# Attention and a two-layer network on one core: a shorter float64 conversion, unread matmuls, and four instead of eight weight pieces in float32

## The chip, the core and the metric

The kernel runs on one core of a Trainium2 chip. The metric is the device time of one execution in microseconds. Engines are named as the profile names them: PE is TensorE (PEld its weight loads), DVE is VectorE, ACT is ScalarE, POOL is GpSimd, SP is SyncE, which issues the transfers.

## The reference

Causal attention over 4 batches, 12 heads, 448 positions and 64 columns a head, and then a two-layer network on its output, 1792 tokens of 768 columns, with 2048 hidden columns. The two weight matrices are given in float64, the rest in float32; the output is float32.

```python
scores = q @ k.transpose(0, 1, 3, 2) / sqrt(64)
scores = where(triu(ones((448, 448)), k=1), -1e9, scores)
attn = exp(scores - max(scores)); attn = attn / (sum(attn) + 1e-9)
x = (attn @ v).transpose(0, 2, 1, 3).reshape(1792, 768)
h = x @ w_in                                   # w_in  768 x 2048, float64
g = where(h > 0, h, exp(minimum(h, 0)) - 1)
out = (g @ w_out).astype(float32)              # w_out 2048 x 768, float64
```

## The kernel before

The 448 positions of each batch are cut into four chunks of 112. Tile g is chunk g of all four batches, 448 tokens. The kernel goes through the four tiles: the two layers of tile g run on PE interleaved with the attention of tile g + 1, in proportion to their costs. Only the attention of tile 0 (`first_pair`) stands alone, at the start. It goes by six pairs of heads. For each pair, scores of both heads go into two PSUM tiles `sc`; DVE adds the mask and finds the row's extreme (L267); ACT takes the exponential (L271); DVE or POOL multiplies by the reciprocal of the sum (L352); PE transposes the result into a PSUM tile `tr` (L286); ACT or DVE copies that to `at` (L289, L290); PE multiplies with v into the PSUM tile `av` (L299).

The layers want x as the sum of two float32r parts. `split_x` makes `xh`, a copy on ACT (L314), and `xl`, the rest, on DVE (L316). Weights are cut into 34 pieces: 16 of w_in (768 elements a partition) and 18 of w_out (12 of 768 and 6 of 512). In tile 0, `weights` loads a piece as 64-bit words and converts it: ACT takes the absolute value of the high half (L545), DVE bounds and scales it (L546), DVE masks the sign (L549), DVE shifts and ors (L552), ACT scales the low half (L556), POOL adds the two as integers (L559). The float32 piece `w` is written to DRAM (L562), from where the later tiles load it. Then it is split into two float32r parts, `wh` by a copy on ACT (L571) and `wl` by a subtraction on DVE or POOL (L572), and a product is three matmuls (L581 to L583: high x high, high x low, low x high). In tile 0 the first `PLAIN` = 8 pieces of w_in are not split: they meet an unsplit copy `xf` of x in one float32 matmul (L597). Between the layers, ACT and DVE form g and split it (L604 to L610); L627 copies an output tile out of PSUM.

Buffers come from rings: four PSUM tiles of tag `p` (for `sc` and `tr`), one of tag `av`, three of tag `hp` (both layers); in SBUF eight of tag `w6` (64-bit words, split weights, and from tile 2 on split q and k) and five of tag `w`. In each ring the n-th tile takes the place of the one n - bufs before it, once that is read for the last time. `Ring.free_at` gives tiles out in the order in which they were asked for, except under tag `p`.

The order of all work is found ahead of time by a list scheduler in the kernel's own Python (`Plan`). `add` records an instruction or a lump of them, with the tiles that it reads and writes, an estimated cost, and for some a second or third engine that may do it. PE's lumps carry due times; those of other work follow backwards from what needs it, transfers with a lead that grows with their size. `run` then starts, again and again, the work that can start first, the earliest due among those within 0.12 us, and takes another engine when that would end sooner by the estimates. Each engine thus has one fixed order on the chip; the estimates decide that order and nothing else.

Of the kernel before, what the change touches and what calls it, by code (L numbers as in the profile page):

```python
# [11 lines left out]
U32 = mybir.dt.uint32  # L12
# [5 lines left out]
CP = 112  # L18
# [50 lines left out]
class Plan:  # L69
# [4 lines left out]
    def __init__(self):  # L74
        self.works = []

    def add(self, ways, reads=(), writes=(), due=None, size=0.0, hold=()):


        if isinstance(ways, tuple):  # L80
            ways = [ways]
        full = lambda x: [(b, None) if isinstance(b, Buf) else b for b in x]
        reads, writes = full(reads), full(writes)
        w = Work(ways, size, due, reads, writes, hold)
        meet = lambda a, b: a is None or b is None or a == b
        for b, key in reads:
            w.preds |= {o for o, k, wr in b.uses if wr and meet(k, key)}
        for b, key in writes:
            w.preds |= {o for o, k, wr in b.uses if meet(k, key)}
        for b, key in reads:  # L90
            b.uses.append((w, key, False))
        for b, key in writes:
            b.uses.append((w, key, True))
        for b in w.bufs:
            b.left += 1
        for p in w.preds:
            p.succs.append(w)
        self.works.append(w)
        return w
# [87 lines left out]
def attention_moe_kernel(ctx, tc, qk, v, w_in, w_out, out):  # L187
# [27 lines left out]
    def f32(ap):  # L215
        return ap.bitcast(F32)
# [9 lines left out]
        nm=4, su=4, rr=4, hp=3, p=4, av=1,  # L226
    )

    PLAIN = 8

    SPLIT = 2

# [2 lines left out]
        ring = rings.setdefault(tag, Ring(BUFS[tag], in_order=tag != "p"))  # L235
        return ring.new(lambda: pool.tile(shape, dtype, tag=tag, name=name or tag, bufs=BUFS[tag]))

    def pe(cost, fn, reads, writes, due, hold=()):
        plan.add(("PE", cost, fn, False), reads, writes, due, hold=hold)

    def act(n, fn, more=0.05):
        return ("ACT", more + 0.84e-3 * n, fn, False)
# [4 lines left out]
    def pool(n, fn, rate=2.3e-3):  # L247
        return ("POOL", 0.1 + rate * n, fn, True)

    def dma(kb, rows, fn, reads, writes):  # L250
        plan.add(("SP", 0.35 + 0.5e-3 * rows, fn, False), reads, writes, size=kb / 260.0)

# [12 lines left out]
    def softmax(sc, a, key, c, n, nm, su, x, sums=True):  # L265

        plan.add(dve(n, lambda: nc.vector.tensor_tensor_reduce(  # L267
            out=a()[:, c], in0=sc()[:, c], in1=mask[:, S - n:], op0=ALU.add, op1=ALU.min,
            scale=-scale, scalar=3.0e38, accum_out=nm()[:, x:x + 1],
        )), [(sc, key)], [(a, key), (nm, x)])  # L270
        plan.add(act(n, lambda: nc.scalar.activation(  # L271
            a()[:, c], a()[:, c], AF.Exp, bias=nm()[:, x:x + 1], scale=-1.0, accum_out=su()[:, x:x + 1] if sums else None,
        ), 0.28 if sums else 0.11), [(nm, x)], [(a, key)] + [(su, x)] * sums)

    def reciprocals(su, rr):
        plan.add(dve(4, lambda: nc.vector.tensor_scalar_add(rr(), su(), EPS), more=0.2), [su], [rr])
        plan.add(dve(4, lambda: nc.vector.reciprocal(rr(), rr()), more=0.21), [], [rr])

    def transposes(blocks, due):

        tr, at = new("p", [CP, S], name="tr"), new("at", [CP, S])
        w = CP * len(blocks)

        def fn():
            for x, (a, i) in enumerate(blocks):
# [17 lines left out]
        pe(0.2 * len(what), fn, [vb] + [at for two in what for _, at, _ in two], [(av, b)], due)  # L303

    def split_x(g, p, av):
        if g == 0:
            x = xf[p] = new("gl" if p % 2 else "gh", [P, S], name="xf")
            plan.add([
                act(S, lambda: nc.scalar.activation(x(), av(), AF.Copy)),
                dve(S, lambda: nc.vector.tensor_copy(x(), av())),  # L310
            ], [av], [x])
        xh = new("xh", [P, S], F32R)
        xl = new("xl", [P, S], F32R)
        plan.add(act(S, lambda: nc.scalar.activation(xh(), av(), AF.Copy)), [av], [xh])  # L314
        plan.add(
            dve(S, lambda: nc.vector.tensor_tensor(out=xl(), in0=av(), in1=f32(xh()), op=ALU.subtract)), [av, xh], [xl]  # L316
        )
        xt[g, p] = xh, xl

    first = [(new("gh", [P, S], name="q0"), new("gl", [P, S], name="k0")) for _ in range(NP)]  # L320

    def first_pair(p, due):
        q0, k0 = first[p]
        v0 = new("v", [CP, B, 2, D], name="v0")
        for t, x in enumerate((q0, k0)):
            src = qk[:, 2 * p:2 * p + 2, :, t, :CP].rearrange("b h d c -> (h d) b c")
            dma(224, P * B, lambda x=x, src=src: nc.sync.dma_start(
                out=x().rearrange("p (b c) -> p b c", b=B), in_=src
            ), [], [x])
        for half in range(2):  # L330
            src = v[:, p, :, half, 0].rearrange("b c d -> c b d")
            dma(112, CP * B, lambda half=half, src=src: nc.sync.dma_start(out=v0()[:, :, half], in_=src), [], [(v0, half)])
        sc = [new("p", [CP, S], name="sc") for _ in range(2)]
        a = [new("a", [CP, S]) for _ in range(2)]
        nm, su, rr = (new(x, [CP, 2 * B]) for x in ("nm", "su", "rr"))

        def scores():
            for b in range(B):
                for half in range(2):
                    d = half_of(half)  # L340
                    nc.tensor.matmul(sc[half]()[:, chunk(b)], q0()[d, chunk(b)], k0()[d, chunk(b)], start=True, stop=True)
        pe(0.9, scores, [q0, k0], sc, due, [*a, nm, su, rr])
        for half in range(2):
            for b in range(B):
# [12 lines left out]
        at = [transposes([(a[half], b) for b in range(B)], due + 3.0) for half in range(2)]  # L357
# [170 lines left out]
    def weights(g, key):  # L528
# [7 lines left out]
        if g == 0:  # L536
# [4 lines left out]
            wf = lambda: w()[:, :n]  # L541
            dma(n * P, P, lambda: nc.sync.dma_start(
                out=r()[:, :n].rearrange("p k c w -> p k (c w)"), in_=src.bitcast(U32)
            ), [], [r])
            plan.add(act(size, lambda: nc.scalar.activation(wf(), f32(high()), AF.Abs)), [(r, 1)], [w])  # L545
            plan.add(dve(size, lambda: nc.vector.tensor_scalar(  # L546
                wf(), wf(), MOST, REBIAS, op0=ALU.min, op1=ALU.mult
            ), 0.55e-3, 0.06, True), [], [w])
            plan.add(dve(size, lambda: nc.vector.tensor_scalar(  # L549
                high(), high(), 0x80000000, None, op0=ALU.bitwise_and  # L550
            ), 0.55e-3, 0.06, True), [], [(r, 1)])
            plan.add(dve(size, lambda: nc.vector.scalar_tensor_tensor(  # L552
                out=wf().bitcast(U32), in0=wf().bitcast(U32), scalar=3, in1=high(),
                op0=ALU.logical_shift_left, op1=ALU.bitwise_or,
            ), port=True), [(r, 1)], [w])
            plan.add(act(size, lambda: nc.scalar.activation(  # L556
                low().bitcast(I32), low(), AF.Copy, scale=2.0 ** -29
            )), [], [(r, 0)])
# [3 lines left out]
            dma(n * 64, P, lambda: nc.sync.dma_start(out=k(), in_=wf()), [w], [k])  # L562
        else:
            k = kept[key]
            dma(n * 64, P, lambda: nc.sync.dma_start(out=w()[:, :n], in_=k()), [k], [w])
        if g == 0 and key[0] == "i" and key[1] < PLAIN:
            wt[(g, *key)] = (w,)
            return
        t = whl[key] if g == 0 else new("w6", [P, 2, KT, P], F32R, "whl")
        wh, wl = (lambda: t()[:, 0]), (lambda: t()[:, 1])  # L570
        plan.add(act(size, lambda: nc.scalar.activation(wh()[:, :n], w()[:, :n], AF.Copy)), [w], [(t, 0)])  # L571
        sub = lambda eng: lambda: eng.tensor_tensor(  # L572
            out=wl()[:, :n], in0=w()[:, :n], in1=f32(wh()[:, :n]), op=ALU.subtract
        )
# [63 lines left out]


    FIRST, EACH, SLOW, TAIL = 4.0, 3.0, 1.3, 5.0  # L640
    for p in range(NP):
        first_pair(p, FIRST + EACH * p)
    t = FIRST + EACH * NP + 4.0
# [49 lines left out]
```

## Time and profile before

| what | us |
|---|---|
| median of 3 runs | 675.41 |
| the three runs | 675.42, 673.94, 675.41 |
| the profiled execution | 673.43 |
| its span, first to last instruction | 671.6 |
| PE busy in it | 651.4 (97%) |
| PE weight loads | 552.6 (82%) |
| ACT busy | 457.5 (68%) |
| DVE busy | 437.0 (65%) |
| POOL busy | 132.8 (20%) |

The difference between the time of the profiled execution and its span lies before its first and after its last instruction. Busy times are sums over the whole span; matmuls overlap, and their ends are modelled, so PE's share is not a share of its peak. The mean granted TensorE clock is 0.986 of full speed (2.4 GHz). A float32 matmul shows as two records, a float32r matmul as one.

### The profile page before, as it was taken

The page shows a single profiled execution, that of the slowest core. Times are in us where ns is not written, and L with a number is a line of the kernel's source. Part 1 is how long each engine was busy: PE and PEld are TensorE (multiplying, and loading weights), DVE is VectorE, ACT ScalarE, POOL GpSimd, SP SyncE. Part 2 cuts the span into 40 slices and gives each one's busy share as a digit, 9 for nine tenths or more (in the row PEclk, how much of TensorE's full clock was granted, in tenths as well). Part 3 has the DMA queues.
Part 4 walks back from the last instruction along what each step waited for, and adds up shares of the span by engine and source line. Part 5 has one row for each costly group of instructions (what it writes and reads, how often), then busy time and mean ns, then how long its engine had stood idle before and what let it go on. Part 6 is the DMA issues. An engine that isn't in the chain of part 4 may idle for free.

```text
span 671.6 us, 11799 instructions
## 1 busy us (share of the span) xinstructions
PE 651.4 (97%) x4176; PEld 552.6 (82%) x4176; DVE 437.0 (65%) x998; ACT 457.5 (68%) x1004; POOL 132.8 (20%) x108
## 2 busy tenths in 40 slices
PE   5899999999999999999999999999999999999997
PEld 4655577878888888888888888888888999999996
DVE  5788998999977676875552678677374526554200
ACT  6998888997857888776662788788566436664210
POOL 1343333534341231111020123111111100000000
PEclk9899997999999999999999999999999999999999
DMA  9999566979869353553647446363443643324210
GB/s 231 283 365 354 182 213 172 318 221 280 300 189 300 113 171 87 163 157 106 203 140 212 121 126 191 101 184 109 128 121 104 216 145 94 102 88 115 77 28 27
DMA packets 83578, 114.80 MB, mean 171 GB/s; under 512 B 39104, under 2 KB 59072, under 8 KB 83520
## 3 DMA queue, kind: packets, MB, share of 16 engines
q1 hardware_dynamic: 83520, 114.06, 55.5%
q8 instruction: 33, 0.54, 0.3%
q14 instruction: 25, 0.20, 0.1%
HBM read 95.94 MB, written 18.09 MB: 170 GB/s over the span
## 4 chain that ended last, share of the span: by engine, by line
PE 79%; DVE 9%; ACT 7%; issue 2%; DMA 2%; SPq 0%; ACTq 0%; DVEq 0%
PE op L581 10%; PE hp L581 10%; PE op L583 10%; PE op L582 10%; PE hp L583 10%; PE hp L582 9%; PE av L452 6%; PE tr L473 6%; PE sc L422 4%; ACT a L271 3%; PE hp L597 2%; DVE whl L572 2%; DMA w_o<-w 2%; DVE w L552 1%; DVE w L546 1%
## 5 line engine op out<-in xcount | busy, mean ns | idle before, releaser
L572 DVE TENSOR_TENSOR whl<-w,whl 128x768 fp32r<-128x768 f32 (+1 forms) x114 | 107.0, 941 | 56.6 <-ACT whl L571 53.7
L581 PE MATMUL op<-gh,whl 128*128 128x448 f32 x384 | 143.4, 374 | 0.0
L583 PE MATMUL op<-gh,whl 128*128 128x448 f32 x384 | 140.7, 366 | 1.0 <-DVE whl L572 1.0
L582 PE MATMUL op<-gl,whl 128*128 128x448 f32 x384 | 140.6, 366 | 0.4 <-DVE gl L610 0.4
L571 ACT ACTIVATE whl<-w 128x768 fp32r<-128x768 f32 (+1 forms) x128 | 99.8, 796 | 48.3 <-PE op L583 31.0
L581 PE MATMUL hp<-xh,whl 128*128 128x448 f32 x336 | 127.8, 380 | 0.8 <-ACT whl L571 0.8
L583 PE MATMUL hp<-xh,whl 128*128 128x448 f32 x336 | 124.4, 370 | 1.3 <-DVE whl L572 1.3
L582 PE MATMUL hp<-xl,whl 128*128 128x448 f32 x336 | 124.2, 370 | 0.0
L271 ACT ACTIVATE a<-a,nm 112x112 f32<-112x112 f32 (+3 forms) x192 | 97.1, 520 | 31.3 <-DVE nm L267 31.2
L267 DVE CUSTOM_DVE_ANT_0 a<-sc,mask 112x112 f32<-112x112 f32 (+3 forms) x192 | 75.0, 442 | 42.6 <-PE sc L422 34.7
L559 POOL TENSOR_TENSOR w<-w,w 128x768 int32<-128x768 int32 (+1 forms) x34 | 65.7, 1933 | 98.4 <-DVE w L552 40.0
L581 PEld LDWEIGHTS op<-gh,whl 128*128 128x128 f32 x384 | 72.1, 188 | 9.5 <-issue 3.0
L583 PEld LDWEIGHTS op<-gh,whl 128*128 128x128 f32 x384 | 72.1, 188 | 8.1 <-DVE whl L572 2.0
L582 PEld LDWEIGHTS op<-gl,whl 128*128 128x128 f32 x384 | 72.2, 188 | 6.4 <-DVE gl L610 0.8
L606 DVE SCALAR_TENSOR_TENSOR hp<-m,hp 128x448 f32<-128x448 f32 x64 | 40.1, 627 | 56.0 <-ACT m L605 55.7
L581 PEld LDWEIGHTS hp<-xh,whl 128*128 128x128 f32 x336 | 63.8, 190 | 11.4 <-issue 4.4
L583 PEld LDWEIGHTS hp<-xh,whl 128*128 128x128 f32 x336 | 63.9, 190 | 7.9 <-DVE whl L572 2.1
L582 PEld LDWEIGHTS hp<-xl,whl 128*128 128x128 f32 x336 | 63.9, 190 | 5.3 <-issue 0.2
L604 ACT ACTIVATE m<-hp 128x448 f32<-128x448 f32 x64 | 34.5, 540 | 37.5 <-PE hp L583 36.5
L572 POOL TENSOR_TENSOR whl<-w,whl 128x768 fp32r<-128x768 f32 x14 | 25.9, 1852 | 135.5 <-ACT whl L571 117.8
L452 PEld LDWEIGHTS av<-at,v 112*64 112x64 f32 x864 | 41.6, 137 | 11.9 <-issue 11.0
L452 PE MATMUL av<-at,v 112*64 112x112 f32 x864 | 49.3, 263 | 0.0
(57 smaller groups left out, 859.9 us busy)
## 6 DMA issues: line engine op xcount, KB each, us to landing
w<-w_i SPq DMA_DIRECT2D x48, 384.0 KB, 3.5
w<-w_o SPq DMA_DIRECT2D x36, 384.0 KB, 3.1
w<-in_w_in SPq DMA_DIRECT2D x16, 768.0 KB, 7.7
w<-in_w_out SPq DMA_DIRECT2D x12, 768.0 KB, 5.9
k<-in_qk SPq DMA_DIRECT2D x30, 224.0 KB, 4.1
w_i<-w SPq DMA_DIRECT2D x16, 384.0 KB, 5.0
q<-in_qk SPq DMA_DIRECT2D x24, 224.0 KB, 4.6
out_t<-ob SPq DMA_DIRECT2D x24, 224.0 KB, 2.7
```

The source lines that it names most:

```text
L267: plan.add(dve(n, lambda: nc.vector.tensor_tensor_reduce(out=a()[:, c], in0=sc()[:, c], in1=mask[:, S - n:], op0=ALU.add, op1=ALU.min, sca ...
L271: plan.add(act(n, lambda: nc.scalar.activation(a()[:, c], a()[:, c], AF.Exp, bias=nm()[:, x:x + 1], scale=-1.0, accum_out=su()[:, x:x + 1] ...
L452: nc.tensor.matmul(av()[half_of(half), chunk(o["b"])], o["v"]()[:, half, i], at()[:, chunk(x)], start=i == 0, stop=i == g,)
L473: nc.tensor.transpose(tr()[:, chunk(x)], o["a"][half]()[:, chunk(i)], ident)
L559: plan.add(pool(size, lambda: nc.gpsimd.tensor_tensor(out=wf().bitcast(I32), in0=wf().bitcast(I32), in1=low().bitcast(I32), op=ALU.add)), ...
L571: plan.add(act(size, lambda: nc.scalar.activation(wh()[:, :n], w()[:, :n], AF.Copy)), [w], [(t, 0)])
L572: sub = lambda eng: lambda: eng.tensor_tensor(out=wl()[:, :n], in0=w()[:, :n], in1=f32(wh()[:, :n]), op=ALU.subtract)
L581: nc.tensor.matmul(acc(), wh()[:, k], xh(), start=first, stop=False)
L582: nc.tensor.matmul(acc(), wh()[:, k], xl(), start=False, stop=False)
L583: nc.tensor.matmul(acc(), wl()[:, k], xh(), start=False, stop=last)
L604: plan.add(act(S, lambda: nc.scalar.activation(m(), hp(), AF.Relu, scale=-1.0)), [hp], [m])
L606: plan.add(dve(S, lambda: nc.vector.scalar_tensor_tensor(out=hp(), in0=m(), scalar=-1.0, in1=hp(), op0=ALU.add, op1=ALU.max)), [m], [hp])
```

## The change

Six things change, all but one in the work of tile 0.

- Conversion of the float64 words: DVE clamps the high half to plus or minus `MOST`, ACT scales it with Prelu (positive values by `REBIAS`, negative ones by 2^32 times that, the sign landing in place after the shift), DVE shifts left by three bits. The two instructions for the sign are gone.
- `PLAIN` is 4: pieces 4 to 7 of w_in are split like the others in tile 0.
- The copy `wh` may run on ACT or on DVE, in all tiles.
- `split_x` of tile 0 copies `av` once, to `xf`; `xh` and `xl` are made from `xf`, and `xl` may run on DVE or POOL.
- `fills`: float32 products of the identity with itself into a PSUM tile that the next scores or transposes overwrite. Nothing reads them. Eight stand before the first pair's scores, due two microseconds ahead of them; two before each of the twelve transposes of tile 0, not before that pair's scores (`after`) and due one microsecond ahead of the transposes.
- The planner's estimates: `RATE` 350 for transfers of weights and 280 for others instead of 260 for all, and 0.19 instead of 0.11 us in an exponential without sums.

```diff
-    PLAIN = 8
+    PLAIN = 4
+    RATE = 350.0
...
+    def fills(n, t, due, after=None):
+        for _ in range(n):
+            pe(0.2, lambda: nc.tensor.matmul(t()[:, :CP], ident, ident, start=True, stop=True), [], [t], due, after=after)
+
-    def transposes(blocks, due):
+    def transposes(blocks, due, fill, after):
         tr, at = new("p", [CP, S], name="tr"), new("at", [CP, S])
         w = CP * len(blocks)
+        fills(fill, tr, due - 1.0, after)
...
     def split_x(g, p, av):
...
+        x = xf[p] = new("gl" if p % 2 else "gh", [P, S], name="xf")
+        plan.add([
+            act(S, lambda: nc.scalar.activation(x(), av(), AF.Copy)),
+            dve(S, lambda: nc.vector.tensor_copy(x(), av())),
+        ], [av], [x])
+        plan.add(act(S, lambda: nc.scalar.activation(xh(), x(), AF.Copy)), [x], [xh])
+        sub = lambda eng: lambda: eng.tensor_tensor(out=xl(), in0=x(), in1=f32(xh()), op=ALU.subtract)
+        plan.add([dve(S, sub(nc.vector), port=True), pool(S, sub(nc.gpsimd))], [x, xh], [xl])
...
-        pe(0.9, scores, [q0, k0], sc, due, [*a, nm, su, rr])
+        if p == 0:
+            fills(FILL[0], sc[0], due - 2.0)
+        scored = pe(0.9, scores, [q0, k0], sc, due, [*a, nm, su, rr])
...
-            plan.add(act(size, lambda: nc.scalar.activation(wf(), f32(high()), AF.Abs)), [(r, 1)], [w])
             plan.add(dve(size, lambda: nc.vector.tensor_scalar(
-                wf(), wf(), MOST, REBIAS, op0=ALU.min, op1=ALU.mult
+                wf(), f32(high()), MOST, -MOST, op0=ALU.min, op1=ALU.max
+            ), 0.55e-3, 0.06, True), [(r, 1)], [w])
+            plan.add(act(size, lambda: nc.scalar.activation(wf(), wf(), AF.Prelu, scale=REBIAS, alpha=2.0 ** 32)), [], [w])
+            plan.add(dve(size, lambda: nc.vector.tensor_scalar(
+                wf().bitcast(U32), wf().bitcast(U32), 3, None, op0=ALU.logical_shift_left
             ), 0.55e-3, 0.06, True), [], [w])
-            plan.add(dve(size, lambda: nc.vector.tensor_scalar(
-                high(), high(), 0x80000000, None, op0=ALU.bitwise_and
-            ), 0.55e-3, 0.06, True), [], [(r, 1)])
-            plan.add(dve(size, lambda: nc.vector.scalar_tensor_tensor(
-                out=wf().bitcast(U32), in0=wf().bitcast(U32), scalar=3, in1=high(),
-                op0=ALU.logical_shift_left, op1=ALU.bitwise_or,
-            ), port=True), [(r, 1)], [w])
...
-        plan.add(act(size, lambda: nc.scalar.activation(wh()[:, :n], w()[:, :n], AF.Copy)), [w], [(t, 0)])
+        plan.add([
+            act(size, lambda: nc.scalar.activation(wh()[:, :n], w()[:, :n], AF.Copy)),
+            dve(size, lambda: nc.vector.tensor_copy(wh()[:, :n], w()[:, :n]), 0.55e-3, 0.06, True),
+        ], [w], [(t, 0)])
...
+    FILL = 8, 2
```

## Rows read from the trace of the kernel before

**Rows 1.** Stretches: start:end, length, busy us of five engines, clock, DMA share, GB/s.
```profile
0.00:37.60 37.60, 26.03 (x232) 20.52 (x232) 25.51 (x137) 29.52 (x98) 10.77 (x17) 0.86 1.00 269
37.60:85.40 47.80, 47.80 (x225) 26.04 (x224) 42.27 (x99) 42.22 (x95) 18.87 (x14) 1.00 0.84 294
85.40:130.00 44.60, 42.73 (x245) 35.93 (x244) 42.09 (x79) 38.67 (x80) 19.06 (x10) 0.92 0.71 220
130.00:206.00 76.00, 74.28 (x454) 63.26 (x453) 67.30 (x126) 58.65 (x124) 29.30 (x17) 1.00 0.81 260
206.00:372.00 166.00, 165.24 (x1155) 144.29 (x1153) 103.94 (x251) 114.93 (x266) 27.39 (x25) 1.00 0.53 160
```
**Rows 2.** Chain that ended last, 37 to 75 us: start, us, what.
```profile
48.43 5.28 PE hp L597 x14
53.70 0.94 PE sc L428 x8
...
56.35 0.92 PE av L452 x16
57.27 0.92 PE tr L473 x8
```
**Rows 3.** Timeline of ACT: copies of output tiles, of the first and the last tile.
```profile
206.52 0.55 ACT L627 ACTIVATE ob<-op 128x448 f32<-128x448 f32 x1 [2.14 <-PE op L583]
...
618.44 0.55 ACT L627 ACTIVATE ob<-op 128x448 f32<-128x448 f32 x1 [1.59 <-PE op L583]
...
667.44 0.54 ACT L627 ACTIVATE ob<-op 128x448 f32<-128x448 f32 x1 [9.24 <-PE op L583]
```
**Rows 4.** Groups of PE by line, 85.4 to 206 us: count, busy, mean ns, idle before.
```profile
L452 PE MATMUL av<-at,v 112*64 112x112 f32 x144 | 8.9, 265 | 0.0
L428 PE MATMUL sc<-k,q 64*112 64x224 f32 x56 | 8.3, 377 | 0.9 <-DVE nm L267 0.6 <-ACT at L477 0.3
L473 PE MATMUL tr<-ident,a 112*112 112x112 f32 x64 | 7.8, 265 | 0.0
```
**Rows 5.** Chain that ended last, 0 to 40 us.
```profile
4.72 1.86 PE sc L341 x16
...
7.00 5.31 ACT a L271 x24
...
13.85 0.44 ACT at L289
```
**Rows 6.** Timeline of PE, 102 to 105 us; in brackets idle before and its releaser.
```profile
102.45 0.47 PE L581 MATMUL hp<-xh,whl 128*128 128x448 f32 x1 [0.53 <-ACT whl L571]
...
103.98 0.74 PE L583 MATMUL hp<-xh,whl 128*128 128x448 f32 x1 [0.79 <-DVE whl L572]
```
**Rows 7.** Two short stretches, columns as in rows 1.
```profile
14.00:20.00 6.00, 5.67 (x41) 4.91 (x42) 3.75 (x19) 3.79 (x13) 2.01 (x3) 0.51 1.22 259
104.00:108.00 4.00, 4.00 (x11) 3.61 (x12) 3.96 (x5) 2.26 (x3) 1.91 (x1) 0.50 0.97 365
```
**Rows 8.** Groups by line and shape, 0 to 206 us: conversion, split of weights and x.
```profile
L552 DVE SCALAR_TENSOR_TENSOR w<-w,w 128x768 uint32<-128x768 uint32 x28 | 26.8, 958 | 0.8
L545 ACT ACTIVATE w<-w 128x768 f32<-128x768 f32 x28 | 25.4, 909 | 0.0
L572 DVE TENSOR_TENSOR whl<-w,whl 128x768 fp32r<-128x768 f32 x20 | 21.0, 1049 | 1.1 <-ACT whl L571 0.9
L546 DVE TENSOR_SCALAR w<-w 128x768 f32<-128x768 f32 x28 | 20.3, 724 | 1.9 <-ACT w L545 1.7
L571 ACT ACTIVATE whl<-w 128x768 fp32r<-128x768 f32 x20 | 16.8, 838 | 1.9 <-POOL w L559 1.9
L316 DVE TENSOR_TENSOR xl<-av,xh 128x448 fp32r<-128x448 f32 x12 | 7.4, 619 | 4.0 <-ACT xh L314 2.4 <-PE sc L428 1.5
L314 ACT ACTIVATE xh<-av 128x448 fp32r<-128x448 f32 x12 | 6.5, 539 | 1.8 <-DVE xf L310 1.2 <-PE av L452 0.4 <-PE av L299 0.2
```
**Rows 9.** One line's instructions, whole span: duration ns min/median/max, first and last start.
```profile
L546 DVE TENSOR_SCALAR w<-w x34: 415/554/2209, 29.3 to 198.7; 128x768 f32<-128x768 f32 x28, 128x512 f32<-128x512 f32 x6
```
**Rows 10.** One line's instructions, whole span, as in rows 9.
```profile
L219 ACT ACT_TABLE_LOAD  x1: 1283/1283/1283, 0.7 to 0.7; - x1
```

More of the change, by code (lines that the diff above doesn't have):

```diff
@@ L75, in __init__, with add @@
         self.works = []
-    def add(self, ways, reads=(), writes=(), due=None, size=0.0, hold=()):
+    def add(self, ways, reads=(), writes=(), due=None, size=0.0, hold=(), after=None):
         if isinstance(ways, tuple):
@@ L93, in add @@
             b.uses.append((w, key, True))
+        if after:
+            w.preds.add(after)
         for b in w.bufs:
@@ L236, in new, with pe @@
         return ring.new(lambda: pool.tile(shape, dtype, tag=tag, name=name or tag, bufs=BUFS[tag]))
-    def pe(cost, fn, reads, writes, due, hold=()):
-        plan.add(("PE", cost, fn, False), reads, writes, due, hold=hold)
+    def pe(cost, fn, reads, writes, due, hold=(), after=None):
+        return plan.add(("PE", cost, fn, False), reads, writes, due, hold=hold, after=after)
     def act(n, fn, more=0.05):
@@ L248, in pool, with dma @@
         return ("POOL", 0.1 + rate * n, fn, True)
-    def dma(kb, rows, fn, reads, writes):
-        plan.add(("SP", 0.35 + 0.5e-3 * rows, fn, False), reads, writes, size=kb / 260.0)
+    def dma(kb, rows, fn, reads, writes, rate=280.0):
+        plan.add(("SP", 0.35 + 0.5e-3 * rows, fn, False), reads, writes, size=kb / rate)
     NG = NCH
@@ L272, in softmax @@
             a()[:, c], a()[:, c], AF.Exp, bias=nm()[:, x:x + 1], scale=-1.0, accum_out=su()[:, x:x + 1] if sums else None,
-        ), 0.28 if sums else 0.11), [(nm, x)], [(a, key)] + [(su, x)] * sums)
+        ), 0.28 if sums else 0.19), [(nm, x)], [(a, key)] + [(su, x)] * sums)
     def reciprocals(su, rr):
@@ L305, in split_x @@
     def split_x(g, p, av):
[L306 to L311, printed above, removed]
         xh = new("xh", [P, S], F32R)
         xl = new("xl", [P, S], F32R)
[L314 to L317, printed above, removed]
         xt[g, p] = xh, xl
+        if g:
+            plan.add(act(S, lambda: nc.scalar.activation(xh(), av(), AF.Copy)), [av], [xh])
+            plan.add(dve(S, lambda: nc.vector.tensor_tensor(
+                out=xl(), in0=av(), in1=f32(xh()), op=ALU.subtract
+            )), [av, xh], [xl])
+            return
+        x = xf[p] = new("gl" if p % 2 else "gh", [P, S], name="xf")
[6 more added lines that the diff above has]
+        plan.add([dve(S, sub(nc.vector), port=True), pool(S, sub(nc.gpsimd))], [x, xh], [xl])
     first = [(new("gh", [P, S], name="q0"), new("gl", [P, S], name="k0")) for _ in range(NP)]
@@ L356, in first_pair @@
             plan.add([dve(S, mul(nc.vector), port=True), pool(S, mul(nc.gpsimd), 1.9e-3)], [rr], [a[half]])
-        at = [transposes([(a[half], b) for b in range(B)], due + 3.0) for half in range(2)]
+        at = [transposes([(a[half], b) for b in range(B)], due + 3.0, FILL[1], scored) for half in range(2)]
         av = new("av", [P, S])
@@ L543, in weights @@
                 out=r()[:, :n].rearrange("p k c w -> p k (c w)"), in_=src.bitcast(U32)
-            ), [], [r])
-            plan.add(act(size, lambda: nc.scalar.activation(wf(), f32(high()), AF.Abs)), [(r, 1)], [w])
+            ), [], [r], RATE)
             plan.add(dve(size, lambda: nc.vector.tensor_scalar(
-                wf(), wf(), MOST, REBIAS, op0=ALU.min, op1=ALU.mult
-            ), 0.55e-3, 0.06, True), [], [w])
-            plan.add(dve(size, lambda: nc.vector.tensor_scalar(
-                high(), high(), 0x80000000, None, op0=ALU.bitwise_and
-            ), 0.55e-3, 0.06, True), [], [(r, 1)])
-            plan.add(dve(size, lambda: nc.vector.scalar_tensor_tensor(
-                out=wf().bitcast(U32), in0=wf().bitcast(U32), scalar=3, in1=high(),
-                op0=ALU.logical_shift_left, op1=ALU.bitwise_or,
-            ), port=True), [(r, 1)], [w])
+                wf(), f32(high()), MOST, -MOST, op0=ALU.min, op1=ALU.max
[3 more added lines that the diff above has]
+                wf().bitcast(U32), wf().bitcast(U32), 3, None, op0=ALU.logical_shift_left
+            ), 0.55e-3, 0.06, True), [], [w])
             plan.add(act(size, lambda: nc.scalar.activation(
@@ L561, in weights @@
             )), [(r, 0)], [w])
-            dma(n * 64, P, lambda: nc.sync.dma_start(out=k(), in_=wf()), [w], [k])
+            dma(n * 64, P, lambda: nc.sync.dma_start(out=k(), in_=wf()), [w], [k], RATE)
         else:
             k = kept[key]
-            dma(n * 64, P, lambda: nc.sync.dma_start(out=w()[:, :n], in_=k()), [k], [w])
+            dma(n * 64, P, lambda: nc.sync.dma_start(out=w()[:, :n], in_=k()), [k], [w], RATE)
         if g == 0 and key[0] == "i" and key[1] < PLAIN:
```

## The prediction

> **What bounds the kernel now.** I first cut the span by what TensorE computes. The table of stretches [rows 1] has the first tile's attention (0 to 37.6 us), the eight pieces of w_in that meet x in float32 (to 85.4), the other eight (to 130) and the w_out products with the rest of the second tile's attention (to 206). In the next stretch PE is busy 165.24 of 166.00 us at full clock, and no float64 word is left to convert. The change has nothing to shorten there; I leave 206 to 671.6 alone, and all that follows is about the first 206 us.
>
> "PE busy" is not to be taken at its word, because ends of matmuls are modelled and overlap. A better measure is what the products cost when nothing interrupts them. A float32 product of 448 columns is two records: 14 records in 5.28 us, 0.754 us a product [rows 2]. A three-part product: five output tiles of 16 products lie between the copies at 618.44 and 667.44, so 49.0 / 80 = 0.6125 us [rows 3]. A score record of the second tile costs 0.94 / 8 = 0.1175, a transpose 0.92 / 8 = 0.115, an av record 0.92 / 16 = 0.0575 [rows 2]. Between 85.4 and 206 there are 48 + 96 three-part products, 88.2 us, and by the counts of [rows 4] 56 x 0.1175 + 64 x 0.115 + 144 x 0.0575 = 22.2 of attention; with the last float32 product 111.2 of 120.6 us: PE loses 9.4 there. From 37.6 to 85.4 its row shows no idle at all [rows 1], so I take that stretch as PE-bound. Before 37.6 ACT is busy 29.5 us, nearly all after its first exponential at 7.00 [rows 1, 5]: ACT's queue is the chain.
>
> Where much of the 9.4 went can be seen from 85.4 to 130: DVE is busy 42.1 of 44.6 us, ACT 38.7, the granted clock is 0.92 [rows 1]. At 102 and 104 PE waits for a piece of w_in that ACT and then DVE has just split, and the clock stands at 0.50, the lower level of 1.2 GHz, right behind [rows 6, 7]. DVE sets that stretch, and PE starves.
>
> **The change, part by part.** *Conversion.* Each of 34 pieces (28 of 768 elements, 6 of 512, two thirds of the price) loses one DVE instruction: bound-and-scale, sign mask and shift-or become clamp and shift. The shift-or took 0.958 us [rows 8], so 28 x 0.958 + 6 x 0.64 = 30.7 us leave DVE. Clamp and shift are not in the trace. The nearest row is the bound-and-scale, mean 0.724 us [rows 8], median 0.554 [rows 9]; I price each like the instruction it replaces, so nothing. If one ran at the shift-or's rate it would return 34 x (0.958 - 0.724) = 8 us of DVE, if both 16. Prelu takes Abs's place on ACT, same size, 0.909 us; the other row of that size is 0.838 [rows 8], so nothing, with an end of 2.4 us less and the same more. The chain becomes DVE, ACT, DVE, POOL, one handover more, hidden as long as conversions run a piece ahead; uncovered it costs about one such instruction, 0.9 us.
>
> *PLAIN 8 to 4.* 24 products go from 0.754 to 0.6125: 3.4 us less PE. In return four more pieces are split: 4 x 0.838 on ACT and 4 x 1.049 on DVE [rows 8], 3.4 and 4.2 us. The copy half of a split may now also run on DVE: nearest row 0.554, upper end 0.958.
>
> *One copy out of PSUM.* xh and xl of the first tile are made from SBUF. The single av buffer comes free after one reader instead of three, and the six xh copies (6 x 0.539 = 3.2 us of ACT [rows 8]) need not run before 37.6: only piece 4 needs them. They go into the second stretch; xl (6 x 0.619, 3.7 on DVE) goes with them, or to POOL.
>
> *Unread products.* Eight run before the first scores, while PE waits for q and k until 4.72 [rows 5], and two before each of 12 transposes. Nearest rows: two records like av or like a transpose, 0.115 to 0.23 us a product, twice that at half clock. At 0.23 the 24 are 5.5 us of PE where PE is busy 26.0 of 37.6 [rows 1]: free while PE waits for the softmax, 5.5 if all were on the chain. What they can give: from 14 to 20 us the clock is 0.51, and ACT is busy only 3.79 of 6 [rows 7]: 2.2 us idle while PE works at half rate.
>
> *RATE* changes only the order and lead of weight loads; with no PE idle from 37.6 to 85.4 [rows 1] no load is late now, so nothing.
>
> **The sum.** First stretch: up to 2.2 from the clock and 3.2 from the moved copies; conversions that come earlier will take part of that room, so 2.5 (ends -3.0 and 5.4). From 37.6 to 206, 168.4 us: PE needs 168.4 - 9.4 - 3.4 = 155.6, so at best 12.8 go. ACT would hold 42.2 + 38.7 + 58.7 + 3.4 + 3.2 = 146.2, DVE 42.3 + 42.1 + 67.3 - 30.7 + 4.2 + 3.7 = 128.9. Two engines near 90% in one static order will still make PE wait now and then, as DVE did; I take two thirds, 8.5 (ends 0 and 12.8). Sum 11.0 us.
>
> The profiled execution took 673.43 us, its span 671.6 and 1.8 around it; the median of the runs is 675.41, 2.0 more. 673.4 - 11.0 = 662.4 by the profile, 664.4 by the median: I say 664.
>
> **A rule on ports.** The bound-and-scale has a median of 554 ns and a maximum of 2209 [rows 9]: now and then it stands behind something else. The Trainium skill, GPSIMD Engine Reference, Key points, says that POOL shares its SBUF interfaces with VectorE, and that DVE instructions in a two-port mode, or with two SBUF inputs, contend with it. By that rule copies of w moved to DVE, and xl moved to POOL, would make more such waits. The row gives a price, 2.21 - 0.55 = 1.66 us each; six more of them on the chain would take 10 us and bring the sum to 1. I count as many as now, since the mean of 0.724 already holds them.
>
> **Rivals.**
> 1. *ACT becomes the bound.* From 37.6 to 130, 92.4 us, ACT would hold 42.2 + 38.7 + 3.4 + 3.2 = 87.5. In these two stretches ACT is now filled to 88% and 87% [rows 1]; at that fill 87.5 us take 99. If the copies of w stay on ACT, nothing is won there, 2.5 before and about 1.5 behind: 671. For it: ACT's sum. Against it: the room of 30.7 us on DVE, to which copies may go.
> 2. *PSUM held by the unread products (slower).* They write the transposes' tile, so its buffer is taken right after the pair's scores. The four buffers then hold one pair's scores and transposes, and a later pair's scores wait for the copy out. The first pair takes from 4.72 to 14.29, 9.6 us, from scores to that copy [rows 5], against (37.6 - 7.0) / 6 = 5.1 us a pair now. One pair at a time would add 5 x 4.5 = 22.5 us: 675.4 - 8.5 + 22.5 = 689. It decides from 6.8 us a pair, where 5 x 1.7 eats the other 8.5. Against it: score buffers come free after the masking, so two pairs can be under way.
> 3. *A table load for each Prelu.* The trace has one load, 1.283 us at the start, and none after it [rows 10]. If Prelu and the exponential needed different tables, 34 pieces would load twice: 87 us of ACT, of which its idle time up to 206 (206 - 169 = 37 us) hides some: about 715 to 750. The Trainium skill, ScalarE: Activation LUTs, Table sets, says that functions are loaded in named sets and that a switch costs a load; Prelu is not among the names it lists with exp. Against it: Abs, Relu, Copy and Exp alternate here without a load.
> 4. *All losses go.* 12.8 + 5.4 = 18.2: 657.
>
> **Chances.** Forecast (658 to 669) 0.57; rival 1 (669 to 675) 0.24; rival 2 0.08; rival 3 0.03; rival 4 (under 658) 0.08. A change within 0.3%, 2.0 us, is about what a measurement of this kernel cannot tell from none. Faster takes the forecast, rival 4 and two thirds of rival 1, 0.80; same 0.09; slower 0.11. The range leaves out rivals 2 and 3 and the low tail: 655 to 675.
>
> **What would show it.** Right: no shift-or on DVE, and DVE some 27 us less busy until the last copy of the first tile's output; 48 float32 records, not 96; the first product of w_in near 35 us; no half clock between 14 and 20 us nor near 104; that last copy near 195 instead of 206.52 [rows 3], and the same 465 us behind it. Wrong: ACT full from 35 to 120 us with PE waiting for split pieces (rival 1); scores waiting for copies of transposes (2); more than one table load (3); weights that land late, which would show RATE at fault; or a gain in the first 206 us that is given back behind them.

## The result, and the profile after

The changed kernel took 664.93 us (median; 664.26 to 666.12), the kernel before 675.38 beside it: ratio 0.9861, interval 0.9841 to 0.9881. By the medians that is 10.4 us faster; the ratio, which is not that of these two medians, stands for 9.4 us (8.0 to 10.7). The forecast was 664, from a sum of 11.0. The profiled execution took 665.17, its span 662.8, so by the profiles the gain is 8.3 us (8.8 of span); the rest is where the two profiled executions lie among their runs.

The total fits, but its parts do not, and that is what this section and the next are about. First the page of the changed kernel: busy us and share of the span by engine, and its granted clock in 40 slices.

```profile
PE 647.8 (98%) x4264; PEld 559.9 (84%) x4264; DVE 447.4 (67%) x1030; ACT 420.8 (63%) x954; POOL 130.6 (20%) x100
...
PEclk9899999999999999999999999999999999999999
```

ACT lost 37 us of work and DVE gained 10, though the conversion took some 30 off DVE: 56 of the copies `wh`, 31.6 us of DVE, moved there from ACT over all tiles. Next the copies of output tiles on ACT, which answer to [rows 3]: the last of the first tile, the first and the last of the last.

```profile
200.57 0.53 ACT L644 ACTIVATE ob<-op 128x448 f32<-128x448 f32 x1
...
609.63 0.55 ACT L644 ACTIVATE ob<-op 128x448 f32<-128x448 f32 x1 [1.61 <-PE op L600]
...
658.64 0.54 ACT L644 ACTIVATE ob<-op 128x448 f32<-128x448 f32 x1 [9.24 <-PE op L600]
```

The first tile ends at 200.57 instead of 206.52, 5.95 us sooner, not 11. Behind it stand 462.2 us instead of 465.1: 2.9 us less where the prediction saw nothing. (Some 0.8 of them is work of the second tile that is now done before this line; more on it below.)

Where in the first tile? The table of stretches of the changed kernel, columns as in [rows 1]: to 45 us, to the first w_out product, to the end of the tile, and the next tile.

```profile
0.00:45.00 45.00, 37.97 (x318) 28.83 (x320) 29.48 (x136) 33.72 (x102) 12.68 (x16) 0.92 1.04 308
45.00:125.90 80.90, 77.33 (x473) 60.30 (x470) 72.97 (x173) 77.37 (x176) 35.24 (x20) 1.00 0.77 244
125.90:200.60 74.70, 74.59 (x469) 64.81 (x467) 58.49 (x115) 54.61 (x118) 31.58 (x18) 1.00 0.90 295
200.60:365.20 164.60, 164.60 (x1152) 144.08 (x1150) 110.92 (x263) 104.34 (x252) 26.99 (x24) 1.00 0.50 149
```

PE's need in the third row, by the unit prices of the prediction and the counts of PE's groups of that stretch (which answer to [rows 4]):

```profile
L598 PE MATMUL op<-gh,whl 128*128 128x448 f32 x96 | 36.0, 375 | 0.0
...
L469 PE MATMUL av<-at,v 112*64 112x112 f32 x96 | 5.9, 265 | 0.0
L490 PE MATMUL tr<-ident,a 112*112 112x112 f32 x40 | 4.9, 265 | 0.1
L445 PE MATMUL sc<-k,q 64*112 64x224 f32 x32 | 4.1, 372 | 0.0
L439 PE MATMUL sc<-khl,qhl 64*112 64x336 f32 x12 | 1.2, 328 | 0.0
```

96 x 0.6125 + 96 x 0.0575 + 40 x 0.115 + 32 x 0.1175, and 0.09 for each of the 11 records of the next tile's scores that start before 200.57 (the twelfth starts just behind), make 73.7 of 74.7 us: PE loses 1.0. The same count for every kernel of this study gives the table below: us that PE loses, each record counted once, in the stretch in which it starts, at its price at full clock. So time at the lower clock counts as lost, and so do unread products; first-tile score records are put at half the price of the second tile's. The table is the thread of what follows.

| kernel | 0 to 45 | 45 to first w_out product | w_out products | first tile ends |
|---|---|---|---|---|
| before | 21.2 | 6.5 | 4.2 | 206.5 |
| after | 21.8 | 5.8 | 1.0 | 200.6 |
| e1 after, unread products not issued | 21.8 | 5.8 | 1.0 | 200.6 |
| e2 after, one more DVE instruction | 25.1 | 19.3 | 14.7 | 231.1 |
| e3 after, PLAIN 8 | 21.8 | 1.5 | 6.7 | 205.4 |
| e5 after, old rates | 20.1 | 5.4 | 8.4 | 205.1 |
| e6 after, three copies | 22.1 | 5.7 | 1.9 | 201.6 |
| e7 after, copies on ACT | 21.3 | 3.7 | 2.2 | 199.2 |
| e10 after, clamp not issued | 21.3 | 5.3 | 1.1 | 199.7 |
| e13 after, PLAIN 2 | 22.2 | 11.2 | 4.0 | 207.6 |
| e4 before, conversion | 19.3 | 2.2 | 7.6 | 203.8 |
| e9 before, conversion and PLAIN 4 | 18.7 | 11.2 | 7.8 | 209.0 |
| e11 before, those and the rates | 25.3 | 4.2 | 2.5 | 203.9 |
| e12 before, the rates | 25.0 | 1.1 | 7.7 | 209.1 |

From before to after the losses fall from 31.9 to 28.5, by 3.4 us. Four pieces less in float32 take another 3.4 us off PE's need, and 0.8 us more of the next tile's scores are done before the line. 3.4 + 3.4 - 0.8 = 6.0: these are the 5.95 us of the first tile.

The conversion itself came as priced. Groups by line and shape of the changed kernel, 0 to 200 us:

```profile
L566 ACT ACTIVATE w<-w 128x768 f32<-128x768 f32 x28 | 23.4, 842 | 0.5 <-DVE w L562 0.4
L562 DVE TENSOR_SCALAR w<-w 128x768 f32<-128x768 f32 x28 | 18.9, 683 | 3.1 <-DMA w<-in_w_in 2.5 <-DMA w<-in_w_out 0.6
L567 DVE TENSOR_SCALAR w<-w 128x768 uint32<-128x768 uint32 x28 | 18.3, 654 | 5.4 <-ACT w L566 5.3
L587 DVE CAST whl<-w 128x768 fp32r<-128x768 f32 x5 | 3.7, 741 | 0.7 <-POOL w L573 0.7
```

Clamp and shift cost 0.683 and 0.654 us, a little less than the two instructions that they replaced (the bound-and-scale 0.724 [rows 8], the sign mask 0.673); Prelu 0.842 where Abs cost 0.909 [rows 8]. There is one table load, as before:

```profile
L221 ACT ACT_TABLE_LOAD  x1: 1283/1283/1283, 0.7 to 0.7; - x1
```

### The profile page after: what moved, and what is told of

The parts are those of the page before. It is cut to its first block, busy times and chain, and to the rows that moved or that the text cites. A ratio compares the mean times of both kernels' runs of the same rounds, so it can differ in the third digit from the quotient of the medians.

```text
span 662.8 us, 11878 instructions
## 1 busy us (share of the span) xinstructions
PE 647.8 (98%) x4264; PEld 559.9 (84%) x4264; DVE 447.4 (67%) x1030; ACT 420.8 (63%) x954; POOL 130.6 (20%) x100
## 4 chain that ended last, share of the span: by engine, by line
PE 86%; DVE 5%; ACT 3%; SPq 2%; issue 2%; POOL 1%; DMA 1%; POOLq 0%; ACTq 0%; DVEq 0%
PE op L598 12%; PE op L600 12%; PE op L599 12%; PE hp L598 11%; PE hp L600 10%; PE hp L599 10%; PE av L469 7%; PE tr L490 6%; PE sc L439 5%; SPq L347 1%; PE sc L445 1%; SPq L342 1%; ACT w L566 1%; ACT a L275 1%; DVE whl L589 1%
## 5 line engine op out<-in xcount | busy, mean ns | idle before, releaser
L589 DVE TENSOR_TENSOR whl<-w,whl 128x768 fp32r<-128x768 f32 (+1 forms) x118 | 117.4, 997 | 52.7 <-ACT whl L586 50.6
L598 PE MATMUL hp<-xh,whl 128*128 128x448 f32 x360 | 135.6, 377 | 0.0
L600 PE MATMUL hp<-xh,whl 128*128 128x448 f32 x360 | 131.8, 366 | 2.5 <-DVE whl L589 2.5
L599 PE MATMUL hp<-xl,whl 128*128 128x448 f32 x360 | 131.6, 366 | 0.0
L586 ACT ACTIVATE whl<-w 128x768 fp32r<-128x768 f32 (+1 forms) x76 | 59.8, 792 | 58.0 <-PE op L600 47.3
L271 DVE CUSTOM_DVE_ANT_0 a<-sc,mask 112x112 f32<-112x112 f32 (+3 forms) x192 | 74.7, 443 | 29.9 <-PE sc L439 21.4
L573 POOL TENSOR_TENSOR w<-w,w 128x768 int32<-128x768 int32 (+1 forms) x34 | 63.5, 1872 | 90.6 <-DVE w L567 49.0
L598 PEld LDWEIGHTS hp<-xh,whl 128*128 128x128 f32 x360 | 67.6, 188 | 10.9 <-issue 5.2
L600 PEld LDWEIGHTS hp<-xh,whl 128*128 128x128 f32 x360 | 67.6, 188 | 8.8 <-DVE whl L589 3.2
L599 PEld LDWEIGHTS hp<-xl,whl 128*128 128x128 f32 x360 | 67.7, 188 | 5.2 <-issue 0.2
L589 POOL TENSOR_TENSOR whl<-w,whl 128x768 fp32r<-128x768 f32 (+1 forms) x14 | 24.7, 1766 | 142.7 <-ACT whl L586 92.0
L626 ACT ACTIVATE gh<-hp 128x448 fp32r<-128x448 f32 x64 | 34.4, 538 | 28.2 <-DVE hp L623 28.2
L627 DVE TENSOR_TENSOR gl<-hp,gh 128x448 fp32r<-128x448 f32 x64 | 39.7, 620 | 17.2 <-ACT gh L626 16.8
```

Of the source, the lines that this page charges most:

```text
L271: plan.add(dve(n, lambda: nc.vector.tensor_tensor_reduce(out=a()[:, c], in0=sc()[:, c], in1=mask[:, S - n:], op0=ALU.add, op1=ALU.min, sca ...
L573: plan.add(pool(size, lambda: nc.gpsimd.tensor_tensor(out=wf().bitcast(I32), in0=wf().bitcast(I32), in1=low().bitcast(I32), op=ALU.add)), ...
L589: sub = lambda eng: lambda: eng.tensor_tensor(out=wl()[:, :n], in0=w()[:, :n], in1=f32(wh()[:, :n]), op=ALU.subtract)
L598: nc.tensor.matmul(acc(), wh()[:, k], xh(), start=first, stop=False)
L599: nc.tensor.matmul(acc(), wh()[:, k], xl(), start=False, stop=False)
L600: nc.tensor.matmul(acc(), wl()[:, k], xh(), start=False, stop=last)
```

## The experiments

All were timed beside the kernel before (674.0 to 674.4 us in these sessions). Ratios are to it; the changed kernel's is 0.9861 (0.9841 to 0.9881). "In its own order" means that the planner saw the same work, so only the named instructions differ; in the other kernels it made a new plan. An interval reaches 0.8 to 1.6 us to either side, so two kernels less than about 2 us apart are not told from each other. And each new plan is one plan: how far the time moves from plan to plan by itself was not measured, so a difference between two plans belongs to the edit only as far as the traces show how.

**e1, unread products not issued, own order.**

```diff
-            pe(0.2, lambda: nc.tensor.matmul(t()[:, :CP], ident, ident, start=True, stop=True), [], [t], due, after=after)
+            pe(0.2, lambda: None, [], [t], due, after=after)
```

> The changed kernel in its own order, with the 32 unread products not issued (nothing else is left out; the order was still planned with them). Theory: they cover a time in which PE waits for the softmax, and in the changed kernel PE runs its first av products at half clock in spite of them, so they are worth little: 664.9 plus or minus 2. Rival: they hold the clock up in the first stretch, as the prediction counted (2.2 us): 667 to 670. Second rival: they stand in PE's way: 660 to 662.

663.89 us, ratio 0.9842 (0.9823 to 0.9861); the first tile ends at 200.60 instead of 200.57. The products themselves are worth nothing; if anything they cost a microsecond. From 14 to 17 us the clock stood at 0.52 with them and at 1.00 without, in the profiled executions of the changed kernel and of e1:

```profile
14.00:17.00 3.00, 3.00 (x25) 2.53 (x24) 0.49 (x2) 0.54 (x1) 0.00 (x0) 0.52 1.13 280
```

```profile
14.00:17.00 3.00, 3.00 (x22) 2.62 (x22) 0.00 (x0) 1.00 (x2) 0.00 (x0) 1.00 1.12 288
```

So they did not hold the clock where the prediction wanted it held. These are one execution of each, but over the whole execution the mean granted clock was 0.992 to 0.994 in all four runs with the products and 0.995 to 0.998 in all four without.

**e2, the shift-or's price back on DVE, own order.**

```diff
+                nc.vector.scalar_tensor_tensor(
+                    out=wf().bitcast(U32), in0=wf().bitcast(U32), scalar=0, in1=wf().bitcast(U32),
+                    op0=ALU.logical_shift_left, op1=ALU.bitwise_or,
+                )
```

> The changed kernel in its own order, with one more DVE instruction behind each of the 34 shifts (the piece shifted by nothing and ored with itself, which changes no value and costs what the old shift-or cost, 0.95 us). Theory: DVE's freed 30.7 us are what feeds PE; given back, most of the gain behind 37.6 us goes: 670 to 675, with PE waiting for split pieces between 50 and 130 us. Rival: PE was the bound and DVE had room: at most 667.

694.33 us, ratio 1.0294 (1.0273 to 1.0315), far more than expected. The added line, and the first tile's end in its timeline:

```profile
L571 DVE SCALAR_TENSOR_TENSOR w<-w 128x768 uint32<-128x768 uint32 x28 | 31.3, 1118 | 1.0
```

```profile
231.11 0.53 ACT L650 ACTIVATE ob<-op 128x448 f32<-128x448 f32 x1
```

The tile is 30.5 us longer for 35.5 us more of DVE (34 pieces; the old shift-or took 0.958 us on a large one). Work that the plan doesn't know of costs nearly its whole duration here, although the kernel before has an instruction of that kind in every piece, too, and ends the tile at 206.5. So this is the price of the order more than of the engine: where both are planned anew, the old conversion costs 4.6 us more than the new one (e4 below).

**e10, clamp not issued, own order.** It leaves out the bound for words beyond float32; Prelu then reads the high words directly (that line is not shown).

```diff
-            plan.add(dve(size, lambda: nc.vector.tensor_scalar(
-                wf(), f32(high()), MOST, -MOST, op0=ALU.min, op1=ALU.max
-            ), 0.55e-3, 0.06, True), [(r, 1)], [w])
+            plan.add(dve(size, lambda: None, 0.55e-3, 0.06, True), [(r, 1)], [w])
```

> The changed kernel in its own order with the clamp of the 34 pieces not issued; ACT's Prelu reads the high words directly. What is left out is the bound for words that float32 cannot hold. Theory: DVE sets tile 0, so taking 25 us more off it in the same order shortens tile 0 by another 4 to 8 us, down to where PE alone bounds it: 657 to 661. Rival: one DVE microsecond is worth one microsecond both ways, as giving 34 shift-ors back cost 29 us: 640 to 645. Second rival: PE is already the bound: 663 to 665.

663.70 us, ratio 0.9843 (0.9821 to 0.9865); the tile ends at 199.65. DVE is busy 20 us less until then (141 instead of 161), and that brings 0.9: in the changed kernel's order DVE no longer bounds the tile. The second rival held; the theory fell.

**e4, the conversion alone** (before, with the three instructions of the new conversion, planned anew).

> The kernel before, planned anew with the new conversion of the float64 words and nothing else. Theory: PE's losses from 85 to 206 us came from DVE, so this part alone brings 4 to 7 of the 10.4 us: 668 to 671. Rival: the freed DVE time is worth something only with the earlier splits: 673 to 676.

669.79 us, ratio 0.9915 (0.9892 to 0.9938). As expected. In the table the w_in stretch loses 2.2 instead of 6.5, as the argument on DVE said, but the w_out products lose 7.6 instead of 4.2: a part is given back there. Less than a third of the 6.5 were waits. PE's waits in the kernel before, 45 to 129.4 us (total, times, longest):

```profile
PE hp L583 <- DVE whl L572: 0.8, 1, 0.8
PE sc L428 <- DVE nm L267: 0.6, 1, 0.6
PE hp L581 <- ACT whl L571: 0.5, 1, 0.5
```

Some 2.9 us were the clock behind them, 0.50 from 104 to 108 us [rows 7] and 0.78 in the next four, in which PE is never idle (an estimate: the missing shares times 4 us). In e4 PE waits 1.1 us in this stretch, and the clock stays up. The kernel before, then e4:

```profile
108.00:112.00 4.00, 4.00 (x18) 3.63 (x16) 4.00 (x14) 2.55 (x6) 0.44 (x1) 0.78 0.30 116
```

```profile
45.00:123.20 78.20, 77.07 (x422) 54.14 (x421) 58.01 (x143) 70.60 (x154) 31.86 (x22) 1.00 0.81 268
```

**e9, conversion and PLAIN 4** (before, with these two).

> The kernel before, planned anew with the new conversion and with four pieces of w_in in float32, and with nothing else of the change. Theory: these two parts are the change; the single copy out of PSUM, the unread products, the choice of engine for the copies and the planner's new figures add nothing that can be measured: 664 to 667 (before 674.4 to 675.4). Rival: with the four splits ACT becomes the bound unless copies may move: 669 to 673.

674.79 us, ratio 1.0012 (1.0000 to 1.0025): the two main parts together give nothing. The theory fell and the rival understated it. PE loses 11.2 us before the w_out products and 7.8 in them. Its timeline of PE in the latter:

```profile
185.06 0.47 PE L578 MATMUL op<-gh,whl 128*128 128x448 f32 x1 [2.43 <-ACT whl L568]
...
187.03 0.74 PE L580 MATMUL op<-gh,whl 128*128 128x448 f32 x1 [1.29 <-DVE whl L569]
```

PE waits for pieces of w_out that are split too late.

**e5, the planner's old figures** (after; 260 for all transfers, 0.11).

> The changed kernel, planned anew with the planner's old figures: 260 for all transfers, 0.11 in an exponential without sums. Theory: they move only the order, worth nothing beyond the scatter of plans: 663 to 668. Rival: the early loads that let the first product of w_in start at 23 instead of 38 us come from them, and that start is worth something: 668 to 672.

670.83 us, ratio 0.9955 (0.9938 to 0.9972): the three figures together, of which the prediction looked at RATE and put it at nothing, are worth 5.9 us here. No run separates them. By the planner's own estimate of the end (650.5 us for the changed kernel, 662.8 with the three old figures) RATE alone makes 657.3, the exponential's figure 652.1, the rate of the other transfers 650.7; that is the plan's arithmetic, not a measurement. One and the same w_out piece shows how the figures act. SP issues its load, DVE begins its conversion; first the changed kernel, then e5 (timelines of SP and DVE):

```profile
150.31 0.64 SPq L559 DMA_DIRECT2D w<-in_w_out  x1
...
159.09 1.03 DVE L562 TENSOR_SCALAR w<-w 128x768 f32<-128x768 f32 x1 [0.57 <-DMA w<-in_w_out]
```

```profile
159.45 0.38 SPq L559 DMA_DIRECT2D w<-in_w_out  x1
...
176.21 0.62 DVE L495 COPY at<-tr 112x448 f32<-112x448 f32 x1 [1.31 <-PE tr L490]
176.75 0.55 DVE L562 TENSOR_SCALAR w<-w 128x768 f32<-128x768 f32 x1
```

In the changed kernel DVE is there when the piece lands, 8.8 us after its issue. In e5 it begins 17.3 us after, though loads of this size land in 5.9 us there (median): the plan believes it late, and puts it behind a copy that itself waits for PE. In the plan of e5 the 18 loads of w_out land 13.5 to 19.6 us after their issue and each conversion starts 0.2 to 1.6 us after that; in the changed kernel's plan they land 3.8 to 8.1 us after. The piece shown is the clearest. Over the 18 pieces the mean from issue to conversion is 12.2 against 17.7 us, from landing to conversion 5.3 against 11.8, and the w_out products lose 1.0 against 8.4.

**e12, the rates alone, and e11, conversion, PLAIN 4 and rates** (both on before; the 350 in the calls for weights and the 0.19 of the exponential are not shown):

```diff
-    def dma(kb, rows, fn, reads, writes):
-        plan.add(("SP", 0.35 + 0.5e-3 * rows, fn, False), reads, writes, size=kb / 260.0)
+    def dma(kb, rows, fn, reads, writes, rate=280.0):
+        plan.add(("SP", 0.35 + 0.5e-3 * rows, fn, False), reads, writes, size=kb / rate)
```

> The kernel before, planned anew with the new transfer rates and the 0.19 of the exponential, and nothing else. Theory (new): at 260 the plan takes the transfers of tile 0 for slower than they are, so a w_out piece is converted long after it has landed, and PE waits for it at the end of tile 0; the higher rate takes that wait away. In the kernel before, tile 0 loses only 3.6 us in the w_out products and DVE is full there, so alone it brings 1 to 4 us: 671 to 674. Rival: it needs nothing else, 668 to 670. Second rival: it changes nothing by itself: 674 to 676.

> The kernel before, planned anew with the new conversion, four pieces in float32 and the new rates; without the unread products, the single copy out of PSUM and the choice of engine for the copies wh. Theory: these three are the whole gain, and the missing wait shows as w_out products that lose under 2 us: 664 to 667. Rival: the single copy out of PSUM, which let the first product of w_in start at 23 instead of 35 us, is needed too: 669 to 673.

e12: 676.56 us, ratio 1.0026 (1.0011 to 1.0040), no gain; e11: 668.91, ratio 0.9916 (0.9895 to 0.9937). So the rates do not work by themselves, and with conversion and PLAIN 4 they turn nothing (e9) into 5.4 us, half of the change. Early conversion is not enough, either: in e12 the absolute value of a w_out piece starts 9.1 us after the load's issue (mean; 15.9 in the kernel before), and the w_out products still lose 7.7, with DVE busy 74.4 of their 81.3 us. Both e11 and e12 lose 25 us before 45 instead of 21: the last av products of the first tile come near 45.5 instead of 38 to 39 us. That the weights, due sooner, hold up the pairs is likely, but not shown. PE's waits of e11 in that stretch, total, times, longest:

```profile
PE sc L341 <- DMA k<-in_qk: 6.6, 3, 4.5
PE tr L286 <- DVE nm L267: 3.1, 1, 3.1
```

**e3, PLAIN 8, and e13, PLAIN 2** (after, planned anew, one number changed).

> The changed kernel, planned anew with eight pieces of w_in in float32 instead of four. Theory: PE does 24 x (0.754 - 0.6125) = 3.4 us more work and is the bound: 668.3 (667 to 670). Rival: the four splits that are saved on ACT and DVE are worth as much: 664 to 666.

> The changed kernel, planned anew with two pieces of w_in in float32. Theory: with DVE and ACT relieved and the loads early PE is the bound, so 12 products more at 0.6125 instead of 0.754 bring 1.7 us: 662 to 664. Rival: two splits more, needed sooner, make PE wait at the start: 665 to 669.

e3: 669.41 us, ratio 0.9918 (0.9900 to 0.9937); e13: 671.91, ratio 0.9969 (0.9956 to 0.9982). Eight pieces cost 4.5 us by the medians and 4.8 in the first tile: 3.4 of PE's work and 1.4 of losses. These moved, too: 4.2 us less in the w_in stretch and 5.7 more in the w_out products, where PE waits 2.5 and 0.9 us for the second tile's attention (DVE at L271, ACT at L494) and not for weights. Two pieces cost 7.0, where PE's work alone would have saved 1.7. In e13 PE loses 11.2 us in the w_in stretch. Its longest waits there:

```profile
PE hp L600 <- DVE whl L589: 3.3, 5, 1.8
PE tr L490 <- DVE a L515: 0.8, 1, 0.8
PE hp L598 <- DVE whl L587: 0.7, 1, 0.7
```

Splits needed sooner, from queues with the rest of the conversion in them, are what PE then waits for.

**e7, copies wh on ACT alone** (after, planned anew).

> The changed kernel, planned anew with the copies wh on ACT alone in all tiles. Theory: ACT has room, since it is less busy than DVE in the changed kernel: 664 to 667, and the last tile takes 118.2 us again instead of 117.1. Rival: ACT becomes the bound in tile 0, as the prediction's first rival says: 668 to 672.

664.59 us, ratio 0.9855 (0.9836 to 0.9874). Nothing: ACT has the room, and the prediction's first rival falls. The last tile takes 118.2 us again instead of 117.1, as expected, and the first ends 1.4 sooner.

**e6, three copies out of PSUM** (after, planned anew, xh and xl from av).

> The changed kernel, planned anew with xf, xh and xl of the first tile all made from av in PSUM, as before. Theory: of the parts that the three-part kernel lacks, the unread products and the choice of engine were worth nothing, so its missing 4 us are the single copy: 668 to 671, with the first product of w_in back near 38 us. Rival: the single copy is worth nothing either, and the 4 us are the scatter of plans: 663 to 666.

667.93 us, ratio 0.9903 (0.9879 to 0.9926), 3.0 more than the changed kernel by the medians, 1.1 by the spans (663.9 to 662.8), and the intervals touch. The first product of w_in still starts at 24.4 us, so the single copy is not needed to bring it forward. Neither theory is clean: worth something between 1 and 3 us.

Nothing here beats the changed kernel by more than the measurement can tell.

## Why the prediction was right, and where its steps were not

**What bounds the first tile: right, once.** DVE did starve PE from 85 to 130 us: with the conversion alone that loss went from 6.5 to 2.2 us (e4), most of it the lower clock that followed the waits, for a gain of 4.6 us. But the step "two thirds of the losses go" treated the first tile's losses as one sum that shrinks. They move: with the w_in products sped up, the loss appears in the w_out products, 6.7 to 8.4 us in e3, e4, e5, e9 and e12. For the stretch from 37.6 us on the sum had 8.5 us; from 45 us on the tile gave some 4 of losses and 3.4 of PE's work, less the 0.8 of scores done ahead.

**RATE at nothing: the step that failed.** The argument was that PE showed no idle from 37.6 to 85.4, so no load was late. No weights kept PE waiting because they landed late; the plan took them for late, and queued conversions of landed pieces behind other work. That cost little while DVE was full (e12: no gain alone), and 5.9 us, together with the other two figures, once it was not (e5).

**PLAIN 4: right in size, not in its condition.** 3.4 us were worked out, 4.5 measured (e3), 3.4 of the 4.8 in the first tile as PE's work. Without the new rates the same edit takes back all that the conversion gave (e4 to e9, 5.0 us).

**First 37.6 us: wrong.** 2.5 us were expected from the clock and the moved copies; to 45 us PE loses 21.8 instead of 21.2. From 14 to 20 us the clock is 0.76 instead of 0.51, at 0.52 until 17 and at full speed behind, but the unread products are worth nothing (e1). The other sign on the clock came out: near 104 us it stands at 1.00 instead of 0.50. The sign "first product of w_in near 35" came out at 23.4, and it meant little: the first tile's last av products moved from 38.6 to 44.4 in exchange. The plan moved them, not the products as such, since e1 keeps the start without issuing them. Planning them is enough, with three copies too (e6, 24.4); with neither them nor the single copy e11 starts at 40.3. In the planner's own times the single copy would be enough as well: it starts that product at 25.0 us without the unread products, at 33.7 without both, at 21.3 with both. The plan without the unread products but with all else also ends 2.6 us earlier by its estimate; it was not run, so what they cost as part of the plan stays open.

**206 to 671.6 left alone: wrong by 2.9 us.** Three things make it up. The second tile takes 164.7 instead of 166.4 us. Some 0.8 of that is no gain: 11 records of its scores instead of 2 start before the line (10 or 11 in every kernel with the new rates, 2 with the old). Another 0.8 is two waits of the kernel before for split weights of the second tile, 206 to 235 us:

```profile
PE hp L583 <- DVE whl L572: 0.5, 1, 0.5
PE hp L581 <- ACT whl L571: 0.3, 1, 0.3
```

They are what PE's 165.24 us lacked of 166.00 in the prediction's first paragraph. The last tile takes 117.1 where copies may run on DVE, 118.2 where not (e7). PE waits for nothing there in either. But its w_in records start 0.2027 instead of 0.2067 us after one another, 288 of them; in 40 us of that stretch PE starts 4 more (before, then after):

```profile
557.00:597.00 40.00, 40.00 (x195) 36.34 (x194) 22.87 (x33) 25.43 (x44) 0.00 (x0) 1.00 0.33 101
```

```profile
549.40:589.40 40.00, 40.00 (x199) 37.08 (x198) 29.11 (x44) 18.29 (x33) 0.00 (x0) 1.00 0.33 99
```

Why copies on DVE go with that is open.

**DVE 27 us less until the end of the first tile: 16.** 161 us to the tile's end, against 177. The conversion gave its 30; but the subtractions for `wl` took 7.1 us more (4.2 were priced), copies `wh` 5.5, and 3.4 us of normalisation moved there. ACT is busy 3 us less.

**The rivals.** ACT did not become the bound, even with all copies (e7). Of rival 2 the mechanism shows, without the price: in every kernel planned with the unread products the pairs come two by two (scores at 5.0, 7.9, 17.3, 20.2, 30.2 and 34.0 us in the changed kernel; at 4.7, 7.2, 9.0, 16.9, 22.1 and 23.2 before), and products of w_in fill the room. No table was loaded. Losses were not all won. On the rule on ports: in the first tile 26 DVE instructions instead of 19 took at least 0.4 us more than the shortest of their kind, each of them beside POOL at work, 27 us in all instead of 23. So there were more such waits, but not on the chain, as DVE was no longer the bound (e10).

That the sum held is luck in its parts: 2.9 us behind the tile that nobody foresaw, and 5.9 us from the planner's figures, made up for a first stretch that gave nothing and for parts that work against each other.

Without the clamp DVE has 20 us less to do and the tile hardly moves (e10): what is left, some 22 us before 45 and 6 in the w_in stretch, is not DVE's total work.

## What to carry to other kernels

In a kernel with an order planned ahead, an estimate that is wrong the safe way is not free: a transfer that lands before the plan expects it is used when the plan expects it, and what is queued ahead of its user may wait for PE. When an engine is relieved, recheck the estimates that its load was hiding, and measure the parts of a change in the presence of the others: here conversion alone gave 4.6 us, conversion and PLAIN 4 nothing, rates alone nothing, all three 5.4, and the whole 10.4. Each of these is one plan, and plans scatter by an amount that was not measured. Work added to a finished order costs nearly its full length (e2: 30.5 of 35.5 us), and work taken out of it may give nothing (e10); neither says what an engine's time is worth once the order is made anew.

## What the hardware showed that was not expected

The subtraction that makes xl took 0.619 us on DVE with one operand in PSUM [rows 8]. With both in SBUF the mean of three was 1.169, but that is not a price of the operands: two took as long as before, and one 2.28 us, from 30.00 on, beside an addition on POOL.

```profile
L332 DVE TENSOR_TENSOR xl<-xf,xh x3: 611/617/2278, 30.0 to 45.5; 128x448 fp32r<-128x448 f32 x3
```

```profile
29.69 2.10 POOL L573 TENSOR_TENSOR w<-w,w 128x768 int32<-128x768 int32 x1 [4.97 <-DVE w L567]
```

The subtraction for `wl`, both operands in SBUF, shows it with more cases. Beside POOL, and alone:

```profile
76.89 2.07 POOL L573 TENSOR_TENSOR w<-w,w 128x768 int32<-128x768 int32 x1 [0.83 <-DVE w L567]
77.26 2.52 DVE L589 TENSOR_TENSOR whl<-w,whl 128x768 fp32r<-128x768 f32 x1
...
82.45 0.96 DVE L589 TENSOR_TENSOR whl<-w,whl 128x768 fp32r<-128x768 f32 x1
```

Of the 24 of this size on DVE in the first tile, the 17 with no POOL instruction beside them took 0.926 to 0.959 us, the other seven 0.951 to 2.517. So it is a wait for POOL, not slower operands. That agrees with what the Trainium skill (GPSIMD Engine Reference, Key points) says of DVE instructions with two SBUF inputs and POOL contending for the same interfaces.
